# Transposing a token tile block by block in place, with DMAs through DRAM that put the blocks in order

## The chip, the core and the metric

The kernel runs on one core of one Trainium2 chip. The metric is the device time of one execution in microseconds (us). Of the kernel before there are three runs, and their median counts.

## What is computed

Masked attention for 8 batches, 8 heads, 576 tokens and a head dimension of 64, then a mixing over tokens and a two-layer network over channels:

```
scores = where(mask[h], q @ k.T / 8, -1e9)     # half the heads: the last 32 keys
attn   = softmax(scores)                       # the others: every 4th key, 32 of them
x      = (attn @ v) with the heads side by side        # (8, 576, 512)
u      = x + (x.T @ U @ V).T                   # U: 576 x 32, V: 32 x 576
out    = u + relu(u @ w_ch1) @ w_ch2           # 512 -> 2048 -> 512
```

All of it is float32. The 8 * 576 = 4608 tokens are 36 token tiles of 128 rows; a batch is four and a half of them.

## The kernel before, in words

**Numbers.** [...] To keep the precision, most operands are split into a high part (a rounded copy, made by ScalarE) and a low part (the rest, made by a subtraction on VectorE or GpSimd), and three products are added: high*high, high*low, low*high.

**The network** runs in 12 chunks c of three token tiles (`CT = 3`), the loop at L720. For each of 16 slices f of the hidden layer, `layer1(f)` (L732) makes `ph` with 12 matmuls of 384 columns (four with the high part of u^T, `uth`, and high weights, four with low weights, four with the low part `utl`). ScalarE then writes `hh` = relu(ph) rounded (L743), and VectorE writes the rest, `hl` (L744). `layer2(f - 1)` (L748) adds nine matmuls of 512 columns into three accumulators `acc`: for each tile hh with high weights, hh with low weights, hl with high weights. At a chunk's end VectorE adds x to each `acc` (L780), and the three tiles are written out (L781).

**The transposed input.** `layer1` needs u^T, 512 channels by 384 tokens. `transp(t)` (L558) makes the part of token tile t, at the end of the chunk before: ScalarE copies the transposed tile into `uth` (L571) and VectorE writes the rest into `utl` (L572). There is one `uth` and one `utl`, so these copies can start only when the last `layer1` of the chunk has read them. The transposed tile itself comes from `turn_x(t, r)` (L548) for the tiles 6 to 35: the 32x32 transpose of VectorE (`STREAM_TRANSPOSE`) is used 16 times, each time on 32 partitions and 4 blocks (32x128 elements), and each instruction writes its blocks to the partitions where they belong, in `xt`. The first six tiles are transposed by TensorE.

**The attention** of batch b + 1 and the mixing over tokens run beside the chunks. TensorE makes scores (`s`, L376), VectorE adds the mask and finds the maximum (L404, L407), ScalarE takes the exponential (L411), VectorE transposes the weights p (L437), TensorE multiplies by v (`pv`, L448), VectorE scales into `x` or into `xp` (L476). The second half of the channels goes from `xp` to its token rows by DMAs (L480), five or so per group. `split` makes the parts of x for the mixing, `t_mm` (L516) and `mix` (L540, L542) add the mixed part to x. Only after `mix` of both channel halves is a token tile of x ready to be transposed. q and k come by DMAs into `qkr` (L340), split on ScalarE and GpSimd into `qks` (L351 to L355), fetched four units ahead.

**Order.** Every engine takes its instructions in order. What is written here gives each piece of work a position: a batch's work is spread over one and a half chunks, and `turn_x(t, .)` gets the later of half a chunk before its chunk's start and the end of its batch (L714 to L718). A list scheduler with a timeline model then orders each engine's instructions. All DMAs are issued by SyncE (SP), in order as well; a DMA that waits holds up all that are behind it. A batch ends in the middle or at the end of a chunk, so the tiles become ready in bunches: 6 to 8, then 9 to 12, 13 to 17, 18 to 21, 22 to 26, 27 to 30, 31 to 35. The bunches that start with 13, 22 and 31 become ready just before the chunk that needs their first tiles (chunks 4, 7 and 10).

**Buffers.** `xt` comes from the pool `xpool`, 16 buffers of 128x512 float32 that also hold the x tiles and their split parts.

Of the kernel before, what the change touches and what calls it, by code (L numbers as in the profile page):

```python
# [10 lines left out]
F32 = mybir.dt.float32  # L11
# [5 lines left out]
ALU = mybir.AluOpType  # L17
# [6 lines left out]
WIN = 32  # L24
P = 128
# [5 lines left out]
KC = DM // P  # L31
# [29 lines left out]
FETCH = 5  # L61
POST_AT = 0.7
TAIL = 0.25
TURN_STEP = 0.02
NE = 7
QKB = 3
AHEAD_AT = 0.9
# [27 lines left out]
MASK_AT = (None, -16, 0, 16, 32, 48)  # L95
WIDE_AT = (None, 0, 16, 32, 48)
NEG = -8.0e9


def mask_kind(half, j, kinds=MASK_AT, n=QB):  # L100
# [7 lines left out]
def mask_of(off, n):  # L108
# [3 lines left out]
    if off is not None:  # L112
        ok &= (i >= off) == (c >= off)
    return np.where(ok, 0.0, NEG).astype(np.float32)

# [30 lines left out]
def attention_moe_kernel(ctx: ExitStack, tc: tile.TileContext, qk1, qk2, vv, masks, wide, ident, ut, vt, w1, w2, out):  # L146
    nc = tc.nc

    const = ctx.enter_context(tc.tile_pool(name="const", bufs=1))
    work = ctx.enter_context(tc.tile_pool(name="work", bufs=2))  # L150
    xpool = ctx.enter_context(tc.tile_pool(name="xpool", bufs=NX))
    psum = ctx.enter_context(tc.tile_pool(name="psum", bufs=3, space=bass.MemoryType.PSUM))

    held_w = {}
# [131 lines left out]
    xt = {}  # L286
    def x_tile(t):
        if t not in xt:
            xt[t] = xpool.tile([P, DM], F32, tag="x", name=f"x{t}")
        return xt[t]  # L290
# [254 lines left out]

    turned_x = {}

    def turn_x(t, r):  # L548
        if r == 0:
            turned_x[t] = xpool.tile([P, KC, P], F32, tag="x", name=f"xt{t}")  # L550
        tp = turned_x[t]
        x4 = x_tile(t).rearrange("p (k d) -> p k d", k=KC)
        rs = slice(WIN * r, WIN * (r + 1))
        for k in range(P // WIN):
            ks = slice(WIN * k, WIN * (k + 1))
            nc.vector.transpose(out=tp[ks, :, rs], in_=x4[rs, :, ks])  # L556

    def transp(t):  # L558
        c, i = divmod(t, CT)
        if c not in uts:  # L560
            uts[c] = (work.tile([P, KC, CTOK], F32R, tag="uth", name=f"uth{c}", bufs=1),
                      work.tile([P, KC, CTOK], F32R, tag="utl", name=f"utl{c}", bufs=1))
        uh, ul = uts[c]
        if t in turned_x:
            tp = turned_x.pop(t)
        else:
            tp = psum.tile([P, KC, P], F32, tag="ps", name=f"tp{t}")
            for k in range(KC):
                nc.tensor.transpose(out=tp[:, k, :], in_=x_tile(t)[:, k * P:(k + 1) * P], identity=id_sb)
        cs = slice(i * P, (i + 1) * P)  # L570
        nc.scalar.copy(out=uh[:, :, cs], in_=tp)  # L571
        nc.vector.tensor_tensor(out=ul[:, :, cs], in0=tp, in1=uh[:, :, cs].bitcast(F32), op=ALU.subtract)  # L572

    def batch_items(b):
        held = {}
# [73 lines left out]
        if b == 0:  # L649
            hold = after[0][n + 1:]  # L650
            after[0] = after[0][:n + 1]
            m = n + 1
            mixes = [x for p in zip(hold[1:], after[1][m + 1:]) for x in p]
            turns = [lambda t=t: transp(t) for t in range(CT)]
            cut = 2 * CT
            after[1] = [hold[0]] + after[1][:m + 1] + mixes[:cut] + turns + mixes[cut:]
# [39 lines left out]
    def ahead(stage):  # L696
        if stage == 0:
            nc.sync.dma_start(out=wide_sb, in_=wide)
            for n in range(N2, N2 + QKB):
                fetch(n)  # L700
        else:
            for n in range(N2, N2 + LOOK):
                split_qk(n)
            for n in range(N2 + LOOK, N2 + LOOK + DMA_LOOK):
                fetch(n)

    queue = [(HI1 - MARGIN, lambda: ahead(0)), (AHEAD_AT, lambda: ahead(1))]
# [6 lines left out]
    for t in range(DVE_FROM * CT, NTILE):  # L714
        done = 1.5 * ((P * t + P - 1) // S) - 0.5 - MARGIN
        at_ = max(t // CT - 1 + TURN_AT + TURN_GAP * (t % CT), done)
        queue += [(at_ + TURN_STEP * r, lambda t=t, r=r: turn_x(t, r)) for r in range(P // WIN)]
    queue.sort(key=lambda e: e[0])  # L718

    for c in range(NCHUNK):  # L720
        slots = [0]
        uh, ul = uts.pop(c)
# [38 lines left out]
        for f in range(FC):  # L761
            layer1(f)
            if f < FC - 1:
                slot()
            else:
                for t in more[0:2]:
                    transp(t)
            if f > 0:
                layer2(f - 1)
                if f < FC - 1:  # L770
                    slot()
            for _ in range(W_RATE if c == 0 else 0):
                weight_step(NSMALL, NPIECE)
        for t in more[2:]:
            transp(t)
        layer2(FC - 1)
        for i in range(CT):
            t = c * CT + i
            x = xt.pop(t)
# [81 lines left out]
```

## Time and profile before

| | before |
|---|---|
| runs (us) | 1081.57, 1083.85, 1084.34 |
| median | 1083.85 |
| span of the profiled execution, first to last instruction | 1079.6 |
| own time of the profiled execution | not listed apart; the span is 4.25 below the median |
| mean granted clock of TensorE | 0.968 |
| busy: TensorE matmul, VectorE, ScalarE, GpSimd (us) | 1006.9, 793.5, 407.4, 337.7 |
| moved by DMA | 87.33 MB, 81 GB/s on average |
| `STREAM_TRANSPOSE` of `turn_x` | 480 instructions, 145.2 us, first at 230.6, last at 948.8 |

The profile is of one execution. Busy times are unions of what ran on an engine. PE is TensorE's matmuls, DVE is VectorE, ACT ScalarE, POOL GpSimd, SP the engine that issues DMAs. In a list of instructions in order of time, the bracket at a row's end is how long the engine stood idle before it and which instruction released it. The granted clock (PEclk) is the share of full speed that TensorE was allowed in that stretch.

### The profile page before, as it was taken

How to read it: one execution, taken by the hardware profiler on the slowest of the kernel's cores; microseconds unless marked ns; L12 is line 12 of the kernel's file. 1: busy time of each engine (PE TensorE's matmuls, PEld its weight loads, DVE VectorE, ACT ScalarE, POOL GpSimd, SP SyncE). 2: the span in 40 equal slices, each digit the busy share in tenths (PEclk: the TensorE clock that was granted, in tenths of full speed). 3: DMA queues.
4: the chain of work that ended last, by engine and by line, in shares of the span. 5: the costliest groups of instructions: out<-in, count | busy, mean ns of one | idle time of the engine just before them, and what ended most of it. 6: DMA issues, size and time to landing. Idle time of an engine off the chain costs nothing.

```text
span 1079.6 us, 17590 instructions
## 1 busy us (share of the span) xinstructions
PE 1006.9 (93%) x5304; PEld 896.3 (83%) x5304; DVE 793.5 (73%) x2688; ACT 407.4 (38%) x1225; POOL 337.7 (31%) x533
## 2 busy tenths in 40 slices
PE   6688888999999999998999999998999999699998
PEld 6468776988888988987888898897888998599997
DVE  6999998788589778787668878888858876921211
ACT  5566645434234533433323442543324542111110
POOL 1567766243132521242312441433214331000000
PEclk9679999999999999998999999998999999999999
DMA  9556633222222420331202430332302320000000
GB/s 290 165 195 206 208 108 108 72 79 64 65 58 69 122 66 22 102 90 50 79 23 61 114 93 23 103 87 57 92 9 71 101 76 16 30 1 1 30 1 30
DMA packets 75599, 87.33 MB, mean 81 GB/s; under 512 B 10448, under 2 KB 66320, under 8 KB 75504
## 3 DMA queue, kind: packets, MB, share of 16 engines
q1 hardware_dynamic: 75504, 86.20, 26.8%
q8 instruction: 43, 0.70, 0.3%
q14 instruction: 52, 0.43, 0.1%
HBM read 72.00 MB, written 9.44 MB: 75 GB/s over the span
## 4 chain that ended last, share of the span: by engine, by line
PE 62%; DVE 28%; DMA 4%; issue 3%; ACT 1%; POOL 1%; SPq 0%; DVEq 0%; ACTq 0%; POOLq 0%
PE ph L738 28%; PE acc L755 27%; DVE xt L556 9%; PE pv L448 3%; DVE v L211 2%; PE s L376 2%; DVE hl L744 2%; DVE pt L437 2%; DVE pt L440 1%; DVE v L207 1%; PE t L516 1%; DVE p L407 1%; DVE x L476 1%; DVE x L542 1%; DVE xp L476 1%
## 5 line engine op out<-in xcount | busy, mean ns | idle before, releaser
L755 PE MATMUL acc<-w2h,hh 128*128 128x512 f32 x576 | 229.7, 399 | 6.8 <-ACT hh L743 4.5
L352 POOL TENSOR_TENSOR qks<-qkr,qks 128x160 fp32r<-128x160 f32 x192 | 103.8, 540 | 414.5 <-ACT qks L351 259.1
L755 PE MATMUL acc<-w2h,hl 128*128 128x512 f32 x576 | 208.3, 403 | 23.6 <-DVE hl L744 23.4
L755 PE MATMUL acc<-w2l,hh 128*128 128x512 f32 x576 | 228.0, 396 | 0.0
L744 DVE SCALAR_TENSOR_TENSOR hl<-ph,hh 128x384 fp32r<-128x384 f32 x192 | 106.1, 554 | 145.7 <-ACT hh L743 144.5
L411 ACT ACTIVATE p<-p,nmax 128x160 f32<-128x160 f32 (+1 forms) x288 | 116.8, 406 | 202.1 <-DVE nmax L407 200.2
L743 ACT ACTIVATE hh<-ph 128x384 fp32r<-128x384 f32 x192 | 93.2, 485 | 237.5 <-PE ph L738 233.3
L738 PE MATMUL ph<-uth,w1l 128*128 128x384 f32 x768 | 177.6, 343 | 0.0
L738 PE MATMUL ph<-uth,w1h 128*128 128x384 f32 x768 | 176.9, 346 | 0.2 <-ACT uth L571 0.2
L738 PE MATMUL ph<-utl,w1h 128*128 128x384 f32 x768 | 175.8, 341 | 0.1
L738 PEld LDWEIGHTS ph<-uth,w1h 128*128 128x128 f32 x768 | 141.9, 193 | 16.0 <-ACT uth L571 0.6
L556 DVE STREAM_TRANSPOSE xt<-x 32x128 f32<-32x128 f32 x480 | 145.2, 302 | 11.9 <-PE t L516 4.6
L755 PEld LDWEIGHTS acc<-w2h,hl 128*128 128x128 f32 x576 | 107.1, 191 | 51.7 <-DVE hl L744 32.0
L738 PEld LDWEIGHTS ph<-uth,w1l 128*128 128x128 f32 x768 | 138.4, 191 | 0.9
L738 PEld LDWEIGHTS ph<-utl,w1h 128*128 128x128 f32 x768 | 137.0, 189 | 1.5 <-DVE utl L572 0.5
L437 DVE STREAM_TRANSPOSE pt<-p 32x128 f32<-32x128 f32 x384 | 115.7, 301 | 18.6 <-ACT p L411 13.4
L755 PEld LDWEIGHTS acc<-w2h,hh 128*128 128x128 f32 x576 | 108.9, 189 | 23.9 <-ACT hh L743 5.3
L755 PEld LDWEIGHTS acc<-w2l,hh 128*128 128x128 f32 x576 | 108.8, 189 | 15.3
L351 ACT CAST qks<-qkr 128x288 fp32r<-128x288 f32 x192 | 80.9, 428 | 99.2 <-PE s L376 61.2
L355 POOL TENSOR_TENSOR qks<-qkr,qks 64x128 fp32r<-64x128 f32 x192 | 89.6, 467 | 15.1
L448 PE MATMUL pv<-v,pt 96*128 96x128 f32 x576 | 81.5, 286 | 9.5 <-issue 2.9
L448 PEld LDWEIGHTS pv<-v,pt 96*128 96x128 f32 x576 | 77.4, 200 | 14.4 <-issue 6.0
(68 smaller groups left out, 1098.4 us busy)
## 6 DMA issues: line engine op xcount, KB each, us to landing
qkr<-qk SPq DMA_DIRECT2D x192, 144.0 KB, 2.1
raw<-w SPq DMA_DIRECT2D x26, 512.0 KB, 4.4
v<-vv SPq DMA_DIRECT2D x126, 96.0 KB, 2.1
out<-x SPq DMA_DIRECT2D x36, 256.0 KB, 2.3
qkr<-qk SPq DMA_DIRECT2D x22, 224.0 KB, 4.3
qk<-qk SPq DMA_DIRECT2D x7, 448.0 KB, 7.2
raw<-w SPq DMA_DIRECT2D x12, 256.0 KB, 3.2
x<-xp SPq DMA_DIRECT2D x88, 32.0 KB, 1.9
```

Of the source, the lines that this page charges most:

```text
L211: nc.vector.scalar_tensor_tensor(out=o, in0=hi, scalar=-0x80000000, in1=o, op0=ALU.bitwise_and, op1=ALU.bitwise_or)
L351: nc.scalar.copy(out=t[:, 0:QK2], in_=raw)
L352: nc.gpsimd.tensor_tensor(out=t[:, QK2:], in0=raw[:, P:], in1=t[:, P:QK2].bitcast(F32), op=ALU.subtract)
L355: eng.tensor_tensor(out=t[lo, 0:P], in0=raw[lo, 0:P], in1=t[lo, 0:P].bitcast(F32), op=ALU.subtract)
L411: nc.scalar.activation(out=p_sb[:, u, 0:w], in_=p_sb[:, u, 0:w], func=AF.Exp, bias=nmax[:, u:u + 1], scale=-1.0, accum_out=ssum[:, u:u + 1],)
L437: nc.vector.transpose(out=to[:, :, WIN * (r % 2):WIN * (r % 2 + 1)], in_=p_sb[rs, :, QB * s + WIN * k:QB * s + WIN * (k + 1)])
L448: nc.tensor.matmul(pv[:, u, :], lhsT=pt[:, u, :], rhs=v_sb[:, u % 2, :], start=True, stop=True)
L556: nc.vector.transpose(out=tp[ks, :, rs], in_=x4[rs, :, ks])
L738: nc.tensor.matmul(ph, lhsT=w[:, k, :], rhs=u[:, k, :], start=(n == 0), stop=(n == len(seq) - 1))
L743: nc.scalar.activation(out=hh, in_=ph, func=AF.Relu)
L744: nc.vector.scalar_tensor_tensor(out=hl, in0=ph, scalar=0.0, in1=hh.bitcast(F32), op0=ALU.max, op1=ALU.subtract)
L755: nc.tensor.matmul(acc[i], lhsT=h[:, ss], rhs=w, start=(f == 0 and n == 0), stop=(f == FC - 1 and n == 2))
```

## The change

`turn_x(t)` is now one `STREAM_TRANSPOSE` of the whole tile, 128 partitions by 512 elements. It transposes each 32x32 block where it lies, into a new tile `z` (a ring of two, `ZS = 2`), so that the blocks are right in themselves but stand on the wrong partitions. Four DMAs, one for each 32 partitions, write `z` into a DRAM scratch `zd` (a ring of four) in pieces of 128 elements (512 bytes), and a fifth reads it back into `xt` as 128 rows of 512 elements, with the blocks in order. `xt` comes out with another order of its inner dimensions, which the copies in `transp` follow. The DMAs are issued by SP, like all the others. `dynamic_dma_scratch_size` makes room for `z`; no DMA of this kernel uses what it takes away.

```diff
-TURN_STEP = 0.02
+BLK = P // WIN
+ZS = 2
...
+SCRATCH = 1024
...
+    dram = ctx.enter_context(tc.tile_pool(name="dram", bufs=2, space=bass.MemoryType.DRAM))
...
-    def turn_x(t, r):
-        if r == 0:
-            turned_x[t] = xpool.tile([P, KC, P], F32, tag="x", name=f"xt{t}")
-        tp = turned_x[t]
-        x4 = x_tile(t).rearrange("p (k d) -> p k d", k=KC)
-        rs = slice(WIN * r, WIN * (r + 1))
-        for k in range(P // WIN):
-            ks = slice(WIN * k, WIN * (k + 1))
-            nc.vector.transpose(out=tp[ks, :, rs], in_=x4[rs, :, ks])
+    def turn_x(t):
+        z = work.tile([P, BLK, KC, WIN], F32, tag="z", name=f"z{t}", bufs=ZS)
+        nc.vector.transpose(out=z.rearrange("p b k j -> p k b j"),
+                            in_=x_tile(t).rearrange("p (k b i) -> p k b i", k=KC, b=BLK))
+        zd = dram.tile([BLK, WIN, BLK, KC * WIN], F32, tag="zd", name=f"zd{t}", bufs=2 * ZS)
+        for a in range(BLK):
+            nc.sync.dma_start(out=zd[:, :, a, :].rearrange("b i e -> i b e"),
+                              in_=z[WIN * a:WIN * (a + 1)].rearrange("i b k j -> i b (k j)"))
+        tp = xpool.tile([P, BLK, KC, WIN], F32, tag="x", name=f"xt{t}")
+        nc.sync.dma_start(out=tp.rearrange("p a k j -> p (a k j)"), in_=zd.rearrange("b i a e -> (b i) (a e)"))
+        turned_x[t] = tp.rearrange("p a k j -> p k a j")
...
-        nc.scalar.copy(out=uh[:, :, cs], in_=tp)
-        nc.vector.tensor_tensor(out=ul[:, :, cs], in0=tp, in1=uh[:, :, cs].bitcast(F32), op=ALU.subtract)
+        h, l = uh[:, :, cs], ul[:, :, cs]
+        if len(tp.shape) == 4:
+            h, l = (e.rearrange("p k (a j) -> p k a j", a=BLK) for e in (h, l))
+        nc.scalar.copy(out=h, in_=tp)
+        nc.vector.tensor_tensor(out=l, in0=tp, in1=h.bitcast(F32), op=ALU.subtract)
...
-        queue += [(at_ + TURN_STEP * r, lambda t=t, r=r: turn_x(t, r)) for r in range(P // WIN)]
+        queue.append((at_, lambda t=t: turn_x(t)))
...
-    nc = bacc.Bacc("TRN2", target_bir_lowering=False, num_devices=1)
+    nc = bacc.Bacc("TRN2", target_bir_lowering=False, num_devices=1, dynamic_dma_scratch_size=SCRATCH)
```

The scheduler also places the instructions anew. VectorE's rows before the change, at the end of chunk 9, where the tiles 31 to 35 become ready (`hl9_13` is hl of chunk 9, slice 13; `x31` is token tile 31; `xt31` its transpose; m is the mixed part that L542 adds):

```order
L744 SCALAR_TENSOR_TENSOR hl9_13_10643<-ph9_13_10629,hh9_13_10642 128x384
L542 TENSOR_TENSOR x31_8405<-x31_8405,m7_0_1_10499 64x256
L542 TENSOR_TENSOR x32_9437<-x32_9437,m7_1_1_10510 128x256
L542 TENSOR_TENSOR x33_9563<-x33_9563,m7_2_1_10525 128x256
L556 STREAM_TRANSPOSE xt31_10563<-x31_8405 32x4x32 x5
L556 STREAM_TRANSPOSE xt32_10568<-x32_9437 32x4x32 x12
L556 STREAM_TRANSPOSE xt31_10563<-x31_8405 32x4x32 x3
L556 STREAM_TRANSPOSE xt32_10568<-x32_9437 32x4x32 x4
L744 SCALAR_TENSOR_TENSOR hl9_14_10669<-ph9_14_10655,hh9_14_10668 128x384
L556 STREAM_TRANSPOSE xt33_10949<-x33_9563 32x4x32 x3
```

The same place with the change:

```order
L545 TENSOR_TENSOR x33_9385<-x33_9385,m7_2_1_10327 128x256
L553 STREAM_TRANSPOSE z31_10365<-x31_8263 128x4x4x32
L553 STREAM_TRANSPOSE z32_10374<-x32_9267 128x4x4x32
L752 SCALAR_TENSOR_TENSOR hl9_12_10403<-ph9_12_10389,hh9_12_10402 128x384
L545 TENSOR_TENSOR x34_9485<-x34_9485,m7_3_1_10336 128x256
L545 TENSOR_TENSOR x35_9585<-x35_9585,m7_4_1_10347 128x256
L553 STREAM_TRANSPOSE z33_10735<-x33_9385 128x4x4x32
L553 STREAM_TRANSPOSE z34_10773<-x34_9485 128x4x4x32
L752 SCALAR_TENSOR_TENSOR hl9_13_10429<-ph9_13_10415,hh9_13_10428 128x384
L553 STREAM_TRANSPOSE z35_10814<-x35_9585 128x4x4x32
L752 SCALAR_TENSOR_TENSOR hl9_14_10455<-ph9_14_10441,hh9_14_10454 128x384
L580 TENSOR_TENSOR utl10_10485<-xt30_10255,uth10_10484 128x4x128
```

The mixing stands one to two slices f earlier, 24 transposes between two hl have become two, and z33, z34 and z35, each of which needs one of the two buffers of z back, stand ahead of hl9_13 and hl9_14.

On SP at the same place, before the change, the last moves of x (L480) are followed by the writes of chunk 9's result:

```order
L480 DMA x33_9563<-xp71_10328 32x256
L480 DMA x34_9675<-xp71_10328 16x256
L480 DMA x35_9775<-xp71_10328 32x256
L781 DMA out<-x27_7984 128x512
L781 DMA out<-x28_8098 128x512
```

With the change the stores and the loads of the blocks stand there:

```order
L483 DMA x35_9585<-xp71_10138 32x256
L560 DMA xt30_10255<-zd30_10250 128x512
L557 DMA zd31_10367<-z31_10365 32x4x128 x4
L557 DMA zd32_10376<-z32_10374 32x4x128 x2
L560 DMA xt31_10372<-zd31_10367 128x512
L557 DMA zd32_10376<-z32_10374 32x4x128 x2
L557 DMA zd33_10737<-z33_10735 32x4x128 x2
L560 DMA xt32_10381<-zd32_10376 128x512
L557 DMA zd33_10737<-z33_10735 32x4x128 x2
L557 DMA zd34_10775<-z34_10773 32x4x128 x2
L560 DMA xt33_10742<-zd33_10737 128x512
```

Each xt waits for the four stores of its tile, and the rest of the next tile's stores stands behind it. The ends of chunks 3 and 6 look the same, with loads of q and k for the next batch behind the last stores.

## The prediction

> **What bounds the kernel now.** I began with the page: busy shares and the chain that ended last.
>
> ```profile
> PE 1006.9 (93%) x5304; PEld 896.3 (83%) x5304; DVE 793.5 (73%) x2688; ACT 407.4 (38%) x1225; POOL 337.7 (31%) x533
> ...
> PE 62%; DVE 28%; DMA 4%; issue 3%; ACT 1%; POOL 1%; SPq 0%; DVEq 0%; ACTq 0%; POOLq 0%
> ```
>
> TensorE bounds it, and VectorE holds 28% of the chain. A change on VectorE can only win what TensorE loses by waiting, so next come the tenths of L556's busy time in 40 slices of 27 us, and the busy time by stages.
>
> ```profile
> busy tenths in 40 slices 0000000031121023013031004004131002610000
> ```
>
> ```profile
> core 0: us, PE busy (x) PEld busy (x) DVE busy (x) ACT busy (x) POOL busy (x), PEclk, DMA share, GB/s
> 0.00:216.00 216.00, 176.75 (x940) 152.35 (x941) 190.07 (x587) 118.76 (x361) 118.09 (x122) 0.90 0.55 169
> 216.00:1080.00 864.00, 830.14 (x4366) 743.91 (x4365) 603.39 (x2101) 288.60 (x865) 219.65 (x412) 0.99 0.20 59
> 483.00:497.00 14.00, 8.58 (x33) 7.25 (x32) 12.70 (x46) 3.27 (x11) 0.98 (x2) 0.76 0.19 54
> 737.00:747.00 10.00, 7.70 (x28) 6.82 (x29) 8.92 (x34) 3.27 (x11) 0.97 (x2) 0.66 0.14 41
> 914.00:950.00 36.00, 26.00 (x109) 21.68 (x108) 32.38 (x95) 5.43 (x11) 0.00 (x0) 0.86 0.06 23
> ```
>
> From 216 us on TensorE is idle for 864 - 830.1 = 33.9 us in all. That is the ceiling, plus what a low clock costs in the three short stretches. The 39 us lost before 216 lie ahead of the first L556, in the ninth slice, and of all that is changed. What TensorE waits for from 216 us on, in the view of waits (total, times, longest):
>
> ```profile
> PE acc L755 <- DVE hl L744: 18.8, 15, 2.5
> PE s L376 <- DVE nmax L407: 3.6, 2, 2.5
> PE pv L448 <- DVE nmax L407: 2.7, 2, 1.8
> PE acc L755 <- DVE x L780: 2.2, 1, 2.2
> ```
>
> Together 18.8 + 3.6 + 2.7 + 2.2 = 27.3 us, all of it for VectorE, mostly for hl. What VectorE did instead is seen at the largest of them, in order of time, first VectorE, then TensorE.
>
> ```profile
> 919.55 7.61 DVE L556 STREAM_TRANSPOSE xt<-x 32x128 f32<-32x128 f32 x24
> 927.19 0.56 DVE L744 SCALAR_TENSOR_TENSOR hl<-ph,hh 128x384 fp32r<-128x384 f32 x1
> ```
>
> ```profile
> 927.80 0.96 PE L755 MATMUL acc<-w2h,hl 128*128 128x512 f32 x3 [2.52 <-DVE hl L744]
> 933.23 0.97 PE L755 MATMUL acc<-w2h,hl 128*128 128x512 f32 x3 [1.65 <-DVE hl L744]
> 939.23 0.47 PE L755 MATMUL acc<-w2h,hh 128*128 128x512 f32 x1 [2.21 <-DVE x L780]
> ```
>
> 24 transposes run ahead of one hl, and TensorE waits 2.52 us for it; the three gaps that follow one another here cost 6.4 us.
>
> **What the change removes.** The prices:
>
> ```profile
> L556 DVE STREAM_TRANSPOSE xt<-x 32x128 f32<-32x128 f32 x480 | 145.2, 302 | 11.9 <-PE t L516 4.6
> ...
> L744 DVE SCALAR_TENSOR_TENSOR hl<-ph,hh 128x384 fp32r<-128x384 f32 x192 | 106.1, 554 | 145.7 <-ACT hh L743 144.5
> ...
> L542 DVE TENSOR_TENSOR x<-x,m 128x256 f32<-128x256 f32 x64 | 24.7, 417 | 9.0 <-PE m L540 8.4
> ...
> L572 DVE TENSOR_TENSOR utl<-xt,uth 128x512 fp32r<-128x512 f32 x30 | 20.3, 700 | 5.7 <-PE ph L738 3.2 <-ACT uth L571 2.1
> ```
>
> 145.2 us of L556 go. The 30 whole-tile transposes are in no row of before. Below, one costs what an elementwise pass over 512 elements costs, 0.70 us (L572); above, four times a 128-element one, 1.21 us. Work of 256 elements takes 417 ns and of 512 takes 700, so 1.1 ns an element and 134 ns for an instruction; the 302 ns for 128 elements are near that (134 + 142 = 276), so I take 0.70. VectorE is relieved by 145.2 - 30 * 0.70 = 124 us, or 109 at the upper price. Near the end, 32.4 busy us of 36 lose some 25, since six tiles (29 us) become six z (4.2 us).
>
> Two terms follow. The first is the 27.3 us of waits. The second is the clock, which falls in the three stretches: (1 - 0.76) * 8.58 = 2.1, (1 - 0.66) * 7.70 = 2.6 and (1 - 0.86) * 26.0 = 3.6, together 8.3 us of TensorE's work done slowly. The rows put each low clock right after a cluster of gaps, and I expect it to go with them. So 27.3 + 8.3 = 35.6 us can be won. [...]
>
> **What it adds.** 30 * 5 = 150 DMAs on SP and a wait of VectorE on DMAs. Durations to landing (KB each, median us), and one burst of issues on SP:
>
> ```profile
> qkr<-qk SPq DMA_DIRECT2D x192, 144.0 KB, 2.1
> raw<-w SPq DMA_DIRECT2D x26, 512.0 KB, 4.4
> ...
> out<-x SPq DMA_DIRECT2D x36, 256.0 KB, 2.3
> ...
> x<-xp SPq DMA_DIRECT2D x88, 32.0 KB, 1.9
> ```
>
> ```profile
> 887.56 3.04 SPq L480 DMA_DIRECT2D x<-xp  x5
> ```
>
> An issue takes 3.04 / 5 = 0.61 us. A store of 64 KB in pieces of 512 bytes is in no row; its bounds are 1.9 (x from xp) and 4.4 (512 KB), and I take 2.3, the one write to DRAM there is. The load of 256 KB gets 2.3 as well. A tile alone is then 4 * 0.61 + 2.3 + 2.3 = 7 us from z to xt.
>
> This matters where tiles are needed at once, at the ends of chunks 3, 6 and 9. The steps of TensorE there, and ScalarE's and GpSimd's parts:
>
> ```profile
> 955.97 2.10 PE ph L738 x12
> 958.08 2.06 PE acc L755 x9
> ```
>
> ```profile
> L743 ACT ACTIVATE hh<-ph 128x384 fp32r<-128x384 f32 x192 | 93.2, 485 | 237.5 <-PE ph L738 233.3 <-PE acc L755 3.7
> L355 POOL TENSOR_TENSOR qks<-qkr,qks 64x128 fp32r<-64x128 f32 x192 | 89.6, 467 | 15.1
> ...
> L351 ACT CAST qks<-qkr 128x288 fp32r<-128x288 f32 x192 | 80.9, 428 | 99.2 <-PE s L376 61.2 <-DMA qkr<-qk 19.6 <-issue 10.1
> ```
>
> Count from the start of ph of slice 12. The three mixes (3 * 0.42) follow m in the layer2 before, from -1.0 on, so z31 runs at 0.2 to 0.9, z32 to 1.6. SP issues the four stores of z31 from 0.9; the last, at 2.7, lands at 5.0. Two stores of z32 go meanwhile; xt31 goes at 5.0, the other two stores by 6.2, landed at 8.5; then two of z33; xt32 goes at 8.5 and lands at 10.8; the rest of z33's stores goes by 9.7, landed at 12.0. The ring of two makes z33 wait for z31's stores (5.0), z34 for z32's (8.5), z35 for z33's (12.0). Queued behind z34 on VectorE is hl of slice 13, done at 8.5 + 0.70 + 0.55 = 9.75; behind z35 hl of slice 14, done at 13.25. TensorE needs them four matmuls into their layer2, at 11.6 and 15.7. uth can be written once slice 15's second four matmuls are through, at 14.1. The margins are 1.85, 2.45 and 14.1 - 10.8 = 3.3 us, so the round trip is covered, thinly. At the ends of chunks 3 and 6 the next q and k wait on SP behind 23 issues (20 stores, 3 loads), the last of tile 17's after its z at 12.7, so until 15.1. With 2.1 to land and 0.43 + 2 * 0.47 for the split they are there at 18.6; the scores that need them stand in slice 1 of the next chunk, which begins at 14.8 + 2 * 2.06 + 2.10 = 21 and reaches them at about 22: 3 us to spare. The four bunches inside chunks have a slack of the same kind. For what I can't see of these seven bunches I put 6 us, under one each, and 3.5 us for waits that have other causes or stay.
>
> Edits at nothing: the copies in `transp` read xt in another order but as many elements; the smaller scratch is not used.
>
> **The sum**, on the profiled span: 1079.6 - 35.6 + 3.5 + 6 = 1053.5. The runs' median lies 4.25 above that span, so 1057.8, say 1058.
>
> **The rivals.**
> Round trip too long, the side of slower. If a store takes L instead of 2.3 us, hl of slice 13 moves by 2 and that of 14 by 3 for each us, so from L = 2.3 + 2.45 / 3 = 3.1 TensorE waits. Three bunches lose 3 us and four about 2 for each further us, 17 in all; 4.4 gives 22 us and about 8 of clock, and the sign turns near 4.5. At 5 us the loss is 22 + 0.6 * 17 + 8 = 40 against 32 won (35.6 - 3.5): 1092. For it: the 4.4 of the large transfers. Against: the three rows of up to 256 KB, at 1.9 to 2.3. [...] Chance 0.11.
>
> Half given back on SP. If a store's issue takes longer than 0.61 us, or the loads of xt stand waiting for a buffer, q, k and the moves of x come late. 23 issues at 0.75 us use up the 3 us. Two us in each of six bunches beside attention and 4 of clock cost 16 of the 26 won: 1074; with half of that, 1066. About 1069, chance 0.17.
>
> The clock doesn't come back: it falls in those stretches for a cause other than the gaps, of which none is longer than 2.52 us. Then 8.3 us less are won, 1066. For it only the shortness of the gaps; against it that the clock is low nowhere else after 216 us (0.99 on average). Chance 0.08.
>
> No change. The waits are not the transposes' doing but come from the order, with other work ahead of hl just as long (eight transposes of p, at 302 ns as well, are 2.4 us): 1083. Against it stands the row with 24 in a block; and slice 17 of L556's tenths, without any of it, has TensorE busy throughout:
>
> ```profile
> 432.00:459.00 27.00, 27.00 (x152) 24.95 (x151) 20.71 (x80) 11.53 (x38) 7.95 (x16) 1.00 0.34 102
> ```
>
> Chance 0.06.
>
> **How the numbers follow.** The forecast, 1049 to 1064, has 0.58; the upper price of z and the 6 us decide inside it. All of 35.6 us won would be 1048. The range 1049 to 1080 leaves out no change and slower (0.17) and little below. About 0.3% (3.3 us) can be told from no change here. Faster: 0.58 + 0.17 + 0.08 = 0.83; same 0.06; slower 0.11.
>
> **What would show it.** Right: z at about 0.70 us; VectorE near 670 us busy; TensorE's waits for hl from 216 us on under 8 us; clock near 1.0 in the last third; stores landing by 2.5 us. Wrong: z33 to z35 released by DMAs after more than 3.1 us, with hl behind them late; waits of TensorE on qks; or the same busy TensorE time with new gaps at the ends of chunks 3, 6 and 9.

## The result, and the profile after

The change made the kernel faster than forecast: 1044.36 us (median of 4 runs, 1043.67 to 1045.24) against 1084.09 (4 runs, 1081.57 to 1084.89), a ratio of 0.9637 with a 95% interval of 0.9623 to 0.9652. The forecast was 1058, in a range from 1049 to 1080. The profiled execution took 1044.13 us, of which the span is 1042.3. It is 37.3 us shorter than the span before.

Busy time and the chain of the page after:

```profile
PE 997.2 (96%) x5304; PEld 895.1 (86%) x5304; DVE 669.3 (64%) x2238; ACT 411.3 (39%) x1225; POOL 338.4 (32%) x533
...
PE 81%; DVE 12%; DMA 3%; issue 2%; ACT 1%; SPq 0%; POOL 0%; DVEq 0%; ACTq 0%; POOLq 0%
```

VectorE has 450 instructions and 124 us less, and its share of the chain went from 28% to 12%. The stages of after, then what TensorE waited for from 216 us on (total, times, longest):

```profile
0.00:216.00 216.00, 177.83 (x914) 152.68 (x915) 188.59 (x573) 117.73 (x353) 118.00 (x121) 0.87 0.57 171
216.00:1043.00 827.00, 819.32 (x4391) 742.41 (x4389) 480.74 (x1666) 293.54 (x872) 220.43 (x412) 1.00 0.29 80
...
265.11:1042.30 777.19, 770.21 (x4118) 697.69 (x4116) 443.61 (x1518) 269.66 (x796) 198.12 (x369) 1.00 0.28 78
```

```profile
PE acc L763 <- DVE hl L752: 1.2, 2, 0.6
PE acc L763 <- ACT hh L751: 0.4, 1, 0.4
```

Of 28.3 us of waits after 216 us (27.3 of them in the four rows of before), 1.6 are left, and the clock is 1.00 from there on. Before 216 us the new kernel is a little behind: 914 matmuls against 940, at a clock of 0.87 against 0.90.

**What the new way costs.** VectorE's whole-tile transposes and its waits for the ring of z, then the DMAs (KB each, median us to landing):

```profile
L553 DVE STREAM_TRANSPOSE z<-x 128x512 f32<-128x512 f32 x30 | 20.5, 699 | 21.3 <-DMA zd<-z 20.7 <-issue 0.6
```

```profile
zd<-z SPq DMA_DIRECT2D x120, 64.0 KB, 1.9
xt<-zd SPq DMA_DIRECT2D x30, 256.0 KB, 2.8
out<-x SPq DMA_DIRECT2D x36, 256.0 KB, 2.5
```

z takes 699 ns, where 0.70 us was forecast. A store lands after 1.9 us and the load after 2.8, together 4.7 us where 4.6 was assumed; that the sum is so near is in part luck, since each was assumed at 2.3 and the two errors cancel. VectorE does wait 20.7 us for stores, nine times, but where the forecast followed it, TensorE does not feel it. The end of chunk 9, first VectorE, then SP (a row with x6 or x4 is a burst of issues), then TensorE over the same stretch:

```profile
884.26 1.30 DVE L553 STREAM_TRANSPOSE z<-x 128x512 f32<-128x512 f32 x2
...
888.26 0.71 DVE L553 STREAM_TRANSPOSE z<-x 128x512 f32<-128x512 f32 x1
891.75 0.71 DVE L553 STREAM_TRANSPOSE z<-x 128x512 f32<-128x512 f32 x1 [2.78 <-DMA zd<-z]
892.38 0.52 DVE L752 SCALAR_TENSOR_TENSOR hl<-ph,hh 128x384 fp32r<-128x384 f32 x1
895.01 0.71 DVE L553 STREAM_TRANSPOSE z<-x 128x512 f32<-128x512 f32 x1 [2.11 <-DMA zd<-z]
```

```profile
884.99 2.76 SPq L557 DMA_DIRECT2D zd<-z  x6
888.26 0.34 SPq L560 DMA_DIRECT2D xt<-zd  x1
888.64 1.87 SPq L557 DMA_DIRECT2D zd<-z  x4
891.69 0.34 SPq L560 DMA_DIRECT2D xt<-zd  x1
```

```profile
880.00:898.00 18.00, 18.00 (x94) 16.42 (x94) 7.23 (x14) 1.97 (x4) 0.00 (x0) 1.00 0.45 106
```

The steps stand as they were worked out from the order: two z in 1.3 us, six stores, a load, four stores, a load, and z34 and z35 released by stores with hl behind them. They run a little faster, since a store's issue takes 2.76 / 6 = 0.46 us and not 0.61. z34 was expected 8.3 us after z31 (8.5 - 0.2) and came 7.5 us after it (891.75 - 884.26). TensorE is busy for all 18 us.

**Where the 37.3 us came from.** Counting from the first `uth` copy for chunk 1 (263.79 us before, 265.11 after), the stretch before, and in it the three places with a low clock:

```profile
263.79:1079.60 815.81, 784.86 (x4123) 703.48 (x4121) 560.91 (x1944) 269.52 (x806) 200.20 (x375) 0.99 0.20 58
489.30:495.40 6.10, 4.59 (x13) 4.31 (x14) 5.22 (x19) 1.04 (x4) 0.32 (x1) 0.50 0.22 62
738.90:744.90 6.00, 5.21 (x17) 4.66 (x18) 5.67 (x22) 1.36 (x5) 0.97 (x2) 0.50 0.19 57
939.40:949.10 9.70, 7.53 (x21) 6.09 (x21) 9.30 (x29) 0.00 (x0) 0.00 (x0) 0.51 0.22 82
```

| from the first uth copy on, us | before | after | won |
|---|---|---|---|
| length | 815.8 | 777.2 | 38.6 |
| TensorE idle (length less busy) | 31.0 | 7.0 | 24.0 |
| lost at the low clock: 0.50 * 4.59 + 0.50 * 5.21 + 0.49 * 7.53 | 8.6 | 0 | 8.6 |
| the rest of the busy time | 776.3 | 770.2 | 6.1 |

Before rounding the three gains add up to 38.6. The start is 1.3 us later, so 38.6 - 1.3 = 37.3. The last row was in no view of waits: 6 us of what the profile counts as busy was standing still. It was not more work: if each matmul is given the median distance from its start to the next start, by the kinds of the two, the stretch before holds 761.0 us of work and the one after 761.3. One such place before, in which nothing is marked as a wait:

```profile
516.63 0.39 PE L755 MATMUL acc<-w2h,hh 128*128 128x512 f32 x1
516.86 0.39 PE L755 MATMUL acc<-w2l,hh 128*128 128x512 f32 x1
517.34 0.96 PE L738 MATMUL ph<-utl,w1h 128*128 128x384 f32 x4
```

Matmuls of this kind start 0.23 us apart and are shown as 0.39 us long, since they overlap. Here one starts 0.48 us after the last: 0.25 us of standing still, of which 0.16 is covered by the drawn end of the matmul before.

### The profile page after: what moved, and what is told of

It reads as the page before. It is cut to its first block, busy times and chain, and to the rows that moved or that the text cites. A ratio compares the mean times of both kernels' runs of the same rounds, so it can differ in the third digit from the quotient of the medians.

```text
span 1042.3 us, 17400 instructions
## 1 busy us (share of the span) xinstructions
PE 997.2 (96%) x5304; PEld 895.1 (86%) x5304; DVE 669.3 (64%) x2238; ACT 411.3 (39%) x1225; POOL 338.4 (32%) x533
## 4 chain that ended last, share of the span: by engine, by line
PE 81%; DVE 12%; DMA 3%; issue 2%; ACT 1%; SPq 0%; POOL 0%; DVEq 0%; ACTq 0%; POOLq 0%
PE ph L746 36%; PE acc L763 35%; PE pv L451 5%; PE s L379 3%; DVE v L214 2%; PE t L519 2%; DVE pt L443 2%; DVE v L210 1%; DVE utl L580 1%; PE m L543 1%; DMA raw<-ut 1%; DMA raw<-w 1%; DMA raw<-vt 1%; PE s L390 1%; DVE hl L752 1%
## 5 line engine op out<-in xcount | busy, mean ns | idle before, releaser
L763 PE MATMUL acc<-w2h,hl 128*128 128x512 f32 x576 | 214.2, 399 | 4.5 <-DVE hl L752 4.4
L746 PE MATMUL ph<-uth,w1l 128*128 128x384 f32 x768 | 174.6, 340 | 0.0
L746 PE MATMUL ph<-utl,w1h 128*128 128x384 f32 x768 | 173.4, 339 | 0.0
L746 PEld LDWEIGHTS ph<-uth,w1h 128*128 128x128 f32 x768 | 139.3, 190 | 14.7
L763 PEld LDWEIGHTS acc<-w2h,hh 128*128 128x128 f32 x576 | 108.6, 189 | 20.7 <-ACT hh L751 5.5
L407 DVE TENSOR_TENSOR p<-s,wide_sb 128x160 f32<-128x160 f32 x192 | 60.6, 319 | 49.9 <-PE s L379 48.1
```

The lines of the kernel that those rows point to most:

```text
L407: nc.vector.tensor_tensor(out=p_sb[:, u, :], in0=sp[:, 0:KW], in1=wide_sb[:, kind], op=ALU.add)
L746: nc.tensor.matmul(ph, lhsT=w[:, k, :], rhs=u[:, k, :], start=(n == 0), stop=(n == len(seq) - 1))
L763: nc.tensor.matmul(acc[i], lhsT=h[:, ss], rhs=w, start=(f == 0 and n == 0), stop=(f == FC - 1 and n == 2))
```

## The experiments

The theory, A: VectorE's time at the bunches was the cost, directly and through the clock; the DMAs are hidden. The rivals: B, the gain is the new order of the instructions; C, the round trip costs something that better code could win.

### The DMAs taken away, and alone

The whole-tile transpose goes straight into `xt`, with no scratch:

```diff
-        z = work.tile([P, BLK, KC, WIN], F32, tag="z", name=f"z{t}", bufs=ZS)
-        nc.vector.transpose(out=z.rearrange("p b k j -> p k b j"),
+        tp = xpool.tile([P, BLK, KC, WIN], F32, tag="x", name=f"xt{t}")
+        nc.vector.transpose(out=tp.rearrange("p b k j -> p k b j"),
                             in_=x_tile(t).rearrange("p (k b i) -> p k b i", k=KC, b=BLK))
...
```

> The whole-tile transpose alone: it writes straight into xt, and the stores, the DRAM scratch and the loads are left out, so the blocks stay out of order in the result. Theory A (the gain is VectorE's relief; the DMAs are hidden): 1041 to 1047 us, as with them. Rival C (the round trip and the traffic cost something, and more was won than is seen): 1038 us or less.

Measured: 1043.0 us (4 runs), ratio 0.9622 (0.9608 to 0.9636), against 0.9637 (0.9623 to 0.9652) with the DMAs. By the medians all 150 DMAs and the ring's waits cost 1.4 us, and the two intervals overlap.

The kernel before, with the five DMAs of each tile added, into a scratch that nobody uses:

```diff
+        if r == 0:
+            x5 = x_tile(t).rearrange("p (b e) -> p b e", b=BLK)
...
+            for a in range(BLK):
+                nc.sync.dma_start(out=zd[:, :, a, :].rearrange("b i e -> i b e"), in_=x5[WIN * a:WIN * (a + 1)])
...
+            nc.sync.dma_start(out=z.rearrange("p a k j -> p (a k j)"), in_=zd.rearrange("b i a e -> (b i) (a e)"))
```

> The kernel before, with its 16 transposes per tile, plus five DMAs per tile of the same sizes (four stores of the x tile to the DRAM scratch, one load back into a tile that nobody reads). Theory A: 1081 to 1088 us, as before, since DMAs and SP have room. Rival C: 1092 us or more.

Measured: 1083.55 us (10 runs), ratio 0.9998 (0.9988 to 1.0007). Their transfers and their places on SP cost nothing that can be measured, even beside the old transposes. What a late load would cost this run can't show, since nothing waits for it.

### The ring of z

```diff
-ZS = 2
+ZS = 1
```

> The changed kernel with one buffer of z instead of two, so that each transpose waits for the stores of the one before, 0.7 + 4 * 0.47 + 1.9 = 4.5 us apart. Theory A (hl has enough room behind a waiting transpose): 1043 to 1050 us. Rival D (the wait on the ring is what the change lives by): 1058 us or more, with TensorE waiting for hl at the ends of chunks 3, 6 and 9.

Measured: 1043.95 us (4 runs), ratio 0.9624 (0.9607 to 0.9640). One buffer does as well as two. The waits on the ring lie in VectorE's free time.

### VectorE's time given back

Useless transposes of 32x128 behind each z, as long together as what was saved:

```diff
+    def spend(t, r):
...
+        for k in range(BLK if r < 2 else BLK - 1):
+            ks = slice(WIN * k, WIN * (k + 1))
+            nc.vector.transpose(out=idle_sb[ks], in_=x4[rs, :, ks])
...
+        queue += [(at_ + 0.02 * r, lambda t=t, r=r: spend(t, r)) for r in range(BLK)]
```

> The changed kernel, with 14 transposes of 32x128 per tile added that nobody needs, in the places in the queue that the old ones had: 30 * 14 * 0.302 = 127 us, so VectorE is as busy as before while order of mixing, DMAs and the whole-tile transpose stay. Theory A: the waits for hl come back, 20 to 30 us of them, and the low clock with them: 1072 to 1088 us. Rival B (the gain is the new order of the work, with the mixing earlier): 1044 to 1052 us.

Measured: 1097.09 us (4 runs), ratio 1.0116 (1.0101 to 1.0131): 53 us more than after the change and 13 more than before it, above the expected range. The largest waits of TensorE after 216 us:

```profile
PE s L379 <- DVE nmax L410: 10.5, 13, 2.2
PE acc L772 <- DVE hl L761: 9.2, 8, 1.9
```

The waits are back, but part of the loss lies in the first 216 us (850 matmuls of TensorE by then against 914), where the tiles 6 to 8 come to stand at the end of chunk 0. So the same was done from tile 13 on alone:

```diff
+        if t >= 13:
+            queue += [(at_ + 0.02 * r, lambda t=t, r=r: spend(t, r)) for r in range(BLK)]
```

> After the change, with 14 useless 32x128 transposes for each of the tiles 13 to 35 alone (23 * 14 = 322 at 301 ns, 97 us; VectorE near 766 us busy), so that the first 216 us are as after the change (914 matmuls). Theory A (the gain is VectorE's time at the bunches, the clock with it): most of the gain goes. Before the change these 23 tiles took 23 * 16 * 0.302 = 111 us; with 97 + 16 of them taken again, waits of 15 to 30 us come back behind hl and nmax from 340 us on, with a clock below 0.9 near them: 1070 to 1090. Theory B (the gain is the new order of the instructions, or the reordering of the bunches): 1044 to 1052. If the loss in the run with all tiles came from the first 216 us: below 1060.

Measured: 1079.13 us (5 runs), ratio 0.9953 (0.9937 to 0.9969). TensorE waits again, in the view of waits from 216 us on:

```profile
PE s L379 <- DVE nmax L410: 8.5, 9, 2.2
PE acc L773 <- DVE hl L762: 5.4, 6, 1.7
```

The stage from 216 us on, and the longest of three places with a low clock:

```profile
216.00:1079.00 863.00, 836.84 (x4402) 746.40 (x4400) 579.94 (x1995) 288.65 (x873) 218.50 (x412) 0.99 0.28 77
684.05:690.87 6.82, 5.90 (x17) 4.81 (x17) 6.35 (x20) 1.74 (x6) 2.23 (x4) 0.50 0.23 64
```

34.8 of the 39.7 us are gone, with the whole-tile transposes, the DMAs and the ring left as they are. From 216 us to its end this run is 36.2 us longer than the run after the change. TensorE's idle time there is 25.7 us (26.2 less the 0.5 us behind the span's end) against 7.0, and the three low stretches (13.65 us, half of TensorE's busy time in them) cost 6.3: together 25.0 of the 36.2 by the mechanism of A. The other 11 us are busy time; ten matmuls that it had not done by 216 us (904 against 914) are about 2 of them, and the rest stays open. So 97 us of VectorE's time on the bunches are worth nearly the whole gain. But this run does not by itself rule out B, since the added work also moves the order back. Between the last mixing and the chunk's end, VectorE writes four hl at the ends of the chunks 3, 6 and 9 after the change, 3, 2 and 2 before it, and 4, 3 and 2 here. Nor are the waits at the same instructions as before: more of them are for `nmax`.

### One bunch alone, and all others

Tiles 31 to 35 new, 6 to 30 old (the condition below), and the other way round (`t < 31`):

```diff
-        queue.append((at_, lambda t=t: turn_x(t)))
+        if t >= 31:
+            queue.append((at_, lambda t=t: turn_x(t)))
+        else:
+            queue += [(at_ + 0.02 * r, lambda t=t, r=r: turn_old(t, r)) for r in range(BLK)]
```

> The tiles 31 to 35 take the new way, the tiles 6 to 30 the 16 small transposes of before. Theory A (each bunch wins by itself what VectorE no longer does there): the last bunch, from the uth copies of chunk 10 to those of chunk 11, took 80.0 us before the change and 66.7 after it, and loses nothing at its own place: about 13.3 us of the 39.7 come, 1071 (1068 to 1075), with the waits of before left in the earlier chunks (15 to 20 us in all behind hl and nmax) and a clock of 1.00 from 900 us on. Theory B (the gain comes from the order or from freed buffers all over the kernel): 1050 to 1064, or above 1078.

> The tiles 6 to 30 take the new way, the tiles 31 to 35 the 16 small transposes of before. Theory A: only the last bunch's 13.3 us are lost again: 1058 (1054 to 1061), TensorE's waits near 930 us back at 8 us or so with a clock of 0.5 behind some of them, and none before. The gains of this kernel and of the one with the last bunch alone add up to the whole 39.7 within 3 us. Theory B (the bunches depend on each other): the two gains miss the sum by more than 5 us.

Measured: 1073.19 us (4 runs), ratio 0.9905 (0.9878 to 0.9931), and 1052.64 (4 runs), ratio 0.9713 (0.9684 to 0.9742), against 1082.95 for the kernel before beside them. The gains, 9.8 and 30.3, add up to 40.1, so the bunches do win by themselves. But the last is worth 8 to 10 us and not 13.3. In the run with all but the last bunch, TensorE's waits from 216 us on are these, and 0.2 us for hh:

```profile
PE acc L776 <- DVE hl L765: 5.1, 5, 1.5
PE ph L759 <- DVE utl L590: 2.6, 1, 2.6
```

These 7.9 us are the 8 that were expected, but the clock stays at 1.00 there, where it was expected at 0.5 behind some of them. The 13.3 us held 3.7 us of low clock (0.49 * 7.53), which did not come back. This run also settles B at the last bunch: its order there is that of after the change (four hl at each of the three chunk ends), and the old transposes alone cost 8 to 9 us (1052.64 - 1044.36 = 8.3, or 39.7 - 30.3 = 9.4). The run with the last bunch alone has the order of before (3, 2 and 2), and shows what the new transposes cost in it. VectorE's z31 and z32, ScalarE's third copy into `uth`, and the matmul that needs it:

```profile
918.54 1.30 DVE L553 STREAM_TRANSPOSE z<-x 128x512 f32<-128x512 f32 x2
```

```profile
931.00 0.62 ACT L589 CAST uth<-xt 128x512 fp32r<-128x512 f32 x1 [5.08 <-DMA xt<-zd]
```

```profile
931.67 1.65 PE L759 MATMUL ph<-uth,w1h 128*128 128x384 f32 x4 [3.90 <-ACT uth L589]
```

The third copy is for tile 32, the second of the two that went through DRAM. From the start of z31 to it 12.5 us pass, and TensorE waits 3.90 us for it. That is the wait of the round-trip rival. TensorE had released the first copy at 922.91, only 4.4 us after z31. After the whole change z31 starts at 884.26 and the copies open at 898.63 (ScalarE then is released by TensorE, not by a DMA):

```profile
898.63 1.66 ACT L579 CAST uth<-xt 128x512 fp32r<-128x512 f32 x3 [3.02 <-PE ph L746]
```

There are 14.4 us for the same trip, because the mixing that makes x ready stands one to two slices earlier. That shift, which the order had shown, is part of the gain. The scheduler makes it where VectorE has less to do: with the time given back the order moved back. A slow store had its part too: at this place stores took up to 4.8 us to land with the last bunch alone and up to 2.6 after the whole change. With 2.6 the wait would by estimate be 1.7 us (3.90 less 4.8 - 2.6) instead of 3.90. Behind this wait the clock was at 0.50 for 6.8 us, where 1.00 was expected.

### The round trip made longer

Two copies from DRAM to DRAM between the stores and the load:

```diff
+HOPS = 2
...
+        for hop in range(HOPS):
+            zn = dram.tile([BLK, WIN, BLK, KC * WIN], F32, tag=f"zd{hop}", name=f"zd{hop}_{t}", bufs=2 * ZS)
+            nc.sync.dma_start(out=zn.rearrange("b i a e -> (b i) (a e)"), in_=zd.rearrange("b i a e -> (b i) (a e)"))
+            zd = zn
```

> After the change, with two copies from DRAM to DRAM of 256 KB between the stores and the load of each tile, which lengthens the round trip by two transfers (each at least the 1.9 to 2.8 us of the transfers shown, so 4 to 8 us), and SP waits longer with the next stores, the loads of q and k and the moves of x behind it. Theory A (the round trip is covered, with about 4 us of margin for xt at the ends of the chunks 3, 6 and 9 and a ring wait that reaches z first): waits of TensorE come at the ends of the chunks 3, 6 and 9 and on qks, 3 to 8 us each: 1052 to 1080. Theory C (nothing in the round trip matters at this size): 1043 to 1047.

Measured: 1058.5 us (4 runs), ratio 0.9761 (0.9738 to 0.9784), 14 us more than after the change. A copy landed after 3.2 us (median of 60). The largest waits of TensorE from 216 us on, and ScalarE's row ahead of the second:

```profile
PE ph L751 <- ACT uth L584: 4.5, 3, 2.0
PE s L380 <- DVE x L480: 2.8, 1, 2.8
PE s L380 <- POOL qks L359: 1.6, 1, 1.6
```

```profile
441.12 0.43 ACT L355 CAST qks<-qkr 128x288 fp32r<-128x288 f32 x1 [3.23 <-DMA qkr<-qk]
```

With 6.4 us more, `uth` comes late at the ends of the chunks 3, 6 and 9, and the loads of q and k wait behind the stores on SP, as both rivals said, at 1.2 to 2.8 us each and not the 3 to 8 expected. The wait of 2.8 us for x (L480) belongs to the second kind: ScalarE stands still 3.23 us for `qkr` before it, the exponentials are behind that in its order, and VectorE's transposes of p and its x behind them. A store landed after 2.6 us in this run and the load after 3.0, so the landings add up to 2.6 + 6.4 + 3.0 = 12 us. The round trip was hidden with 4.7 and no longer was with 12.

### The first tiles

Tiles 3 to 5 the new way too (below), then tiles 6 to 8 by TensorE as well (`DVE_FROM = 3`):

```diff
-DVE_FROM = 2
+DVE_FROM = 1
```

> The changed kernel with the tiles 3 to 5 turned in the same way instead of on TensorE. Theory A (TensorE and the end of chunk 0 bind there; 12 TensorE transposes of 0.4 us and the waits for x at 180 to 187 us go): 1036 to 1042 us. Rival (the first 216 us are bound by VectorE and the weights, and the round trip comes too late there): 1044 us or more.

Measured: 1055.32 us (4 runs), ratio 0.9737 (0.9721 to 0.9753): 11 us slower than after the change, so my expectation was wrong. The loss is at the start: by 216 us TensorE has done 833 matmuls against 914.

> After the change, but the tiles 6 to 8 too are transposed by TensorE (12 transposes by matmul more, at under 0.3 us some 3 us of TensorE; their 15 DMAs and 3 z go). After the change the start up to the first uth copy of chunk 1 is 1.3 us later than before and the clock of the first 216 us is 0.87 instead of 0.90, with z6 to z8 at its end. Theory A1 (VectorE and the round trip bind in the first part): the start gains 1 to 4 us against 3 lost: 1040 to 1046. Theory A2 (the first part is bound by other things, the weights and the attention of batch 1): 1045 to 1049.

Measured: 1044.42 us (4 runs), ratio 0.9634 (0.9611 to 0.9658), the same as after the change. The start does twenty more matmuls by 216 us (934 against 914), but by 280 us the lead is eleven (1279 against 1268), no more than the twelve transposes: gain and loss cancel, as A1 had it. No version was found that beats the changed kernel.

### How long a gap lowers the clock

hl computed several times at chosen slices, so that TensorE waits there. First 17 and 24 times alone, and 14 times in four slices in a row:

```diff
+AGAIN = {(10, 3): 17, (10, 10): 24, (11, 3): 14, (11, 4): 14, (11, 5): 14, (11, 6): 14}
...
-            nc.vector.scalar_tensor_tensor(out=hl, in0=ph, scalar=0.0, in1=hh.bitcast(F32),
-                                           op0=ALU.max, op1=ALU.subtract)
+            for _ in range(AGAIN.get((c, f), 1)):
+                nc.vector.scalar_tensor_tensor(out=hl, in0=ph, scalar=0.0, in1=hh.bitcast(F32),
+                                               op0=ALU.max, op1=ALU.subtract)
```

> The changed kernel, with hl of some slices written again and again, so that it comes late: in chunk 10 slice 3 17 times (one gap of TensorE, 1 to 3 us), slice 10 24 times (one gap of 4 to 7 us); in chunk 11 slices 3 to 6 14 times each (four gaps of 1 to 3 us, some 5 us apart). Theory A (gaps in a cluster lower the clock, however short): clock 1.0 after the first, below 1 after the second, below 1 in or after the cluster, where about 3 us of work are lost. [...]

Measured: 1074.54 us (1 run). The gaps were 3.41, 7.55, 5.84 and 5.88 us (the four in a row merged into two), and the clock fell behind each: over the 9 us around them it was 0.81, 0.62, 0.62 and 0.62 on average. Short gaps in a cluster were not tested by it.

Then 15 times each, at a single slice and at every second slice of chunk 11:

```diff
+AGAIN = {(10, 3): 15, (11, 2): 15, (11, 4): 15, (11, 6): 15, (11, 8): 15}
```

> After the change, with hl computed 15 times in place of once in chunk 10 slice 3 (a gap by itself) and in chunk 11 slices 2, 4, 6 and 8 (a cluster). By the run with 17 and 24 repeats each repeat is worth 0.59 us, so each gap should be near 2.2 us, shorter than any in that run. Theory 1 (clusters of gaps as short as those before the change, 1.6 to 2.5 us, lower the clock): the windows of about 9 us behind the second to fourth gap of the cluster show a granted clock of 0.6 to 0.9, the single gap leaves 1.00. [...] Time: about 1044 + 5 * 2.2 = 1055, and by theory 1 some 3 to 7 us more.

Measured: 1058.14 us (1 run). Each gap was expected near 2.2 us; two were of 2.23 (the single one and the first of the cluster), two of 1.64 and the last of 0.98. TensorE's rows behind the single gap and behind one of 1.64 us:

```profile
925.66 1.65 PE L765 MATMUL acc<-w2h,hl 128*128 128x512 f32 x3 [2.23 <-DVE hl L754]
...
1004.18 0.97 PE L765 MATMUL acc<-w2h,hl 128*128 128x512 f32 x3 [1.64 <-DVE hl L754]
```

Three matmuls take 1.65 us behind the gap of 2.23 us, and 0.97 behind that of 1.64. So theory 1 does not hold as stated: a single gap of 2.23 us was enough, and no cluster was needed. Nor did length alone decide. In the run with two more hops a gap of 2.81 us left the clock at 1.00 and one of 1.97 lowered it.

The traces show what did. In each of them the granted clock was 1.00 or 0.50, and it changed only on a grid of 3.41 us that held for the whole execution. Here are steps of that grid. In this run, the step with most of the single gap and the one after it:

```profile
921.93:925.34 3.41, 1.51 (x9) 1.18 (x7) 3.20 (x7) 0.00 (x0) 0.00 (x0) 1.00 0.00 0
925.34:928.75 3.41, 3.08 (x7) 2.48 (x8) 0.83 (x2) 0.49 (x1) 0.00 (x0) 0.50 0.03 7
```

With two more hops, two steps that share the gap of 2.81 us, then the step that holds the whole gap of 1.97 us and the one after it:

```profile
442.77:446.19 3.42, 1.72 (x10) 1.29 (x8) 3.24 (x12) 1.23 (x4) 1.96 (x4) 1.00 0.44 119
446.19:449.60 3.41, 2.30 (x15) 2.07 (x16) 2.21 (x11) 1.58 (x7) 0.00 (x0) 1.00 0.25 78
...
668.06:671.47 3.41, 1.44 (x6) 0.86 (x6) 1.82 (x4) 1.70 (x5) 0.00 (x0) 1.00 0.84 243
671.47:674.88 3.41, 3.41 (x11) 3.22 (x11) 2.62 (x11) 2.30 (x10) 2.86 (x6) 0.50 0.47 136
```

A step went slow when TensorE had been busy for less than about half of the step before: 1.51 and 1.44 us of 3.41 were too little, 1.72 was enough, and so were the 2.11 us of the step with the gap of 1.64. Counted over all 14 traces from 216 us on, each of the 21 full-speed steps with a busy share under 0.46 was followed by a slow one, none of the 3369 with over 0.55, and 3 of the 16 between. So the gap of 2.81 us, split between two steps, did no harm, and a cluster of shorter ones did: in the first run with VectorE's time given back, gaps of 0.68 and 1.30 us in one step (697.73 to 701.14, busy 1.44 us) lowered the clock. Theory 1 was right about clusters such as this one, and wrong about the single gap.

## Why the prediction was wrong

**What was right.** The bound (TensorE, waiting for VectorE), the price of z, the sum of the landing times, the steps at the end of chunk 9, that the waits for hl go, that the clock comes back with them, and that the round trip is covered thinly.

**What failed.** The sum took 35.6 us and gave 9.5 back: "For what I can't see of these seven bunches I put 6 us, under one each, and 3.5 us for waits that have other causes or stay." That step is the miss: 1.6 us of waits are left and no new ones came, so it is 8.9 us of the 13.4 by which the forecast was off. Two terms that the sum put at nothing, 6.1 us of standing still and 4.1 us lost at the start, miss it in opposite directions. Worked out against the two traces:

| term of the sum, us | forecast | measured | difference |
|---|---|---|---|
| waits of TensorE after 216 us that go | 27.3 - 9.5 = 17.8 | 28.3 - 1.6 = 26.7 | 8.9 |
| low clock | 8.3 | 8.6 | 0.3 |
| standing still inside the busy time | 0 | 6.1 | 6.1 |
| the first 264 us, beyond its waits | 0 | -4.1 | -4.1 |
| span | 26.1 | 37.3 | 11.2 |
| median less span | 4.25 | 2.06 | 2.2 |

The -4.1 is what is left of 37.3. The last column without its sum is 11.2 + 2.2; together 13.4 us, which is 1057.8 less 1044.36.

The reserve was a guess, with no row behind it. All that could be followed from the order had come out covered, with margins of 1.85 to 3.3 us, and the reserve then charged each bunch for what had just been worked out to be hidden. The runs without DMAs (1.4 us faster, with overlapping intervals) and with one buffer (no slower) show that next to nothing was owed. The range ended where "All of 35.6 us won would be 1048", but the 6.1 us of standing still lay beyond it. The ceiling was put at the 33.9 us of idle time plus the clock, and the busy time was taken to be work. Six us of it were not.

The 4.25 us between span and median held some 2 us of chance. In every execution of every kernel here for which both are listed, the time is 1.7 to 2.0 us above the span. So the profiled execution before took about 1081.4 us, at the lower end of the runs.

**What was left out.** The start. With the change, the tiles 6 to 8 and their SP work stand at 178 to 192 us, at the end of chunk 0, and that stretch does fewer matmuls at a lower clock. Before, then after:

```profile
170.00:192.00 22.00, 19.14 (x95) 15.89 (x95) 17.84 (x57) 11.22 (x35) 11.51 (x20) 0.92 0.32 98
```

```profile
170.00:192.00 22.00, 17.70 (x76) 14.54 (x76) 17.03 (x49) 9.06 (x27) 10.54 (x17) 0.77 0.49 131
```

It is 76 matmuls at 0.77 where it was 95 at 0.92. With those three tiles back on TensorE the stretch is as it was before the change:

```profile
170.00:192.00 22.00, 19.10 (x97) 15.88 (x96) 17.92 (x57) 11.38 (x35) 12.22 (x21) 0.92 0.33 97
```

Without the DMAs it does 91 at 0.92. So the new way of these tiles, their DMAs above all, is what slows it: by 216 us 20 matmuls are missing against the run with the tiles on TensorE, some 4 us at the 0.19 us that a matmul takes on average (777.2 / 4118, an estimate). The text had said that all before 216 us lies "ahead of the first L556, in the ninth slice, and of all that is changed". That holds for the old instructions, not for the new order. Moving those three tiles back to TensorE wins nothing all the same: by 280 us the lead is no more than the transposes themselves.

**The rivals.** The round trip is too long only where something moves: with two more hops, or with the last bunch alone, it costs 1.2 to 3.9 us at a place. The bound worked out for it, a store of 3.1 us, was passed there (up to 4.8 with the last bunch alone). From 216 us on nothing was given back on SP: no wait of TensorE on `qks` is left. The clock did come back. No change is refuted by 0.9637.

What stays open: how much of the gain at the earlier bunches is the order and how much the transposes' time, since only the last bunch was tried with both; and why VectorE's time given back costs more than it did before. The run with all tiles takes 13 us more than the kernel before, at about the same busy time of VectorE. Its first 216 us explain a part.

## What to carry to other kernels

When the order of the new instructions can be followed and each wait comes out covered, charge only waits that have a row or a step behind them; a reserve for the unseen belongs in the range, not in the sum. TensorE's idle time was not the ceiling of the gain here: matmuls that start 0.23 us apart are drawn 0.39 us long, and 6.1 us of standing still lay inside the busy time. So compare the distance of starts with that of an undisturbed stretch. The block transpose with the reordering left to DMAs cost next to nothing (1.4 us by the medians, with overlapping intervals) where z31 stood 14.4 us ahead of the first copy into `uth`. In the run with the last bunch alone z31 stood only 4.4 us ahead, two tiles in a row took 12.5 us, and TensorE waited 3.90 us.

## What the runs showed of the hardware

- One transpose of 128x512 float32 took 699 ns (mean of 30, after the change), one of 32x128 took 302 ns (mean of 480, before it): a quarter of the partitions and a quarter of the row for 43% of the time. 16 small ones are 4.8 us.
- In the 14 traces the granted clock was 1.00 or 0.50 and changed only on a grid of 3.41 us. From 216 us on, a step with TensorE busy for under 0.46 of it was followed by a slow one (21 of 21), one with over 0.55 never (0 of 3369). A slow step with a busy share over 0.8 was followed by full speed (24 of 24), one under 0.74 by another slow one (13 of 13). So the place of a gap on the grid counted beside its length: with two more hops 1.97 us in one step lowered the clock, 2.81 us across two did not. In the run with 17 and 24 repeats the gaps of 3.41, 5.84, 5.88 and 7.55 us all did.
- After the change 64 KB stores to DRAM in pieces of 512 bytes landed after 1.9 us (median of 120), no later than the writes of out of 256 KB (2.5, median of 36), and SP issued them 0.46 us apart (six in 2.76 us).
